# Reordering the opening of a fused attention and MLP kernel: x tiles first, warm-up at once, q two units ahead

## The chip, the cores and the metric

The kernel runs on one core of a Trainium2 chip. The metric is the device time of one execution in microseconds (us). A profile's span is some 1.8 us shorter than the time of the same execution (573.3 against 575.08 us before the change). Names: PE is TensorE (PEld its weight loads), DVE is VectorE, ACT is ScalarE, POOL is GpSimd, SP is SyncE, which here issues nearly all DMAs.

Each run reports its mean granted clock: 0.997 on a 573 us span means about 3.4 us at half rate, and the profile of the kernel before, with 0.997, has one such stretch of 3.41 us in its middle. The mean takes what comes before the first recorded change of the clock in a run as 1.00, even where the durations of the matmuls show half rate: in the kernel before the first change is at 13.42 us, and the stretch from 10.75 to 13.33 us reads 1.00 with its matmuls at 107 ns, against 55 ns later.

## The reference, cut to what matters

```python
mod = (silu(c) @ w_mod)              # six rows of 512: sa, ca, ga, sb, cb, gb
h = layernorm(x) * (1 + ca) + sa     # x: 2048 x 512
q = h @ wq                           # 32 heads of 128, 8 kv heads
p = softmax(q @ k.T * 128**-0.5)     # over the last 512 keys of the cache
x = x + ga * ((p @ v) @ wo)
h = layernorm(x) * (1 + cb) + sb
x = x + gb * (relu(h @ w1) @ w2)     # hidden size 1792
```

Inputs and output are bfloat16. The work is cut into 128 units: 4 blocks of 512 rows times 32 heads.

## The kernel before

In the timelines each engine starts its instructions in the order of the program text (PE before the change: column matmuls at 9.76 us, warm block at 10.61, then transposes and groups of four warm matmuls in turn from 13.13). The parts that the change and the argument touch:

```python
def warm(n):                          # matmuls on an identity tile, result unused
    for i in range(n):
        mm(bank[WBK][:, :P], ident[:, :], ident[:, :], True, True, [R_ident], [WBK], i == n - 1)

# --- opening ---
dma(c_col[:, :], c[0].rearrange("(c p) -> p c", p=P), "c", writes=[R_c], eng=ACT)
load_wm(1, ACT)                       # w_mod, two slices of 512 KB, on ACT's queue
load_wm(0, ACT)
for t in range(TPB):                  # four x tiles of 128 KB, on SP's queue
    dma(x_sb[:, t, :], xv[:, t, :], f"xa{t}", writes=[R_x[t]])
load_wq(0, 2)
load_k(0)
# ... POOL: ones, ident, constants; load_v(0); load_wq(2, 2)
silu()                                # DVE works on c first
for t in range(TPB):
    ln_stat(t)
ln_rstd(0)                            # one power on POOL for four tiles
for f in mod_cols_mm(0, QBK):         # 32 matmuls with one column each: silu(c) @ w_mod
    f()
mod_cols_evac(0, QBK)
warm(24)
for tl in range(TPB):
    ln_norm(tl)
    ln_tposes(tl, [0, 2])             # PE transposes of the normalized tile
    if tl < TPB - 1:
        warm(4)
ln_mod_ps([0, 2], hT[0], R_hT[0], 1)  # hT = xn.T * (1 + ca) + sa, on DVE and ACT
# ... more loads
q_mms(0)

# --- background loads, by step ---
add(60, load_w1)
add(64, load_w2)                      # two DMAs of 896 KB

# --- steady state ---
for s in range(NU):
    run_tasks(s, 100)
    # ... 
    s_mms(s, 0)                       # scores of unit s, first half; exp on ACT
    if s + 1 < NU:
        q_mms(s + 1)                  # q of the next unit; copy to qT on ACT
    s_mms(s, 1)
    if s >= 1:
        pv_mms(s - 1)                 # p @ v; DVE normalizes to o; DMA transposes o to oT
    pop_bg(4)                         # four matmuls of the output projection oT @ wo
```

## Time and profile before

| | value |
|---|---|
| time before the change | 574.68 us (573.48 to 574.73, 3 runs) |
| span of the profiled run | 573.3 us |
| PE busy | 551.1 us, 96% |
| first matmul | 9.76 us |
| first score matmul | 17.71 us |

The page of the kernel before. The first line is busy time, share and instruction count by engine. The other two show 40 slices of the span, in tenths: PE's busy share and the clock granted to it.

```profile
PE 551.1 (96%) x4082; PEld 316.8 (55%) x4157; DVE 242.8 (42%) x531; ACT 347.7 (61%) x445; POOL 38.2 (7%) x40
...
PE   3899999999999999989999999999999999999997
...
PEclk9999999999999999989999999999999999999999
```

PE is the bound (96% busy), and it is idle mainly at the start, up to 9.76 us. The table of waits, for PE (engine, tile, line, released by what: us in total, times, longest):

```profile
PE psQ L1350 <- DMA wmw<-in_w_mod_dram: 9.8, 1, 9.8
PE psW L1350 <- DMA oT<-o: 2.5, 1, 2.5
PE psS L1350 <- ACT qT L1455: 1.1, 2, 0.8
PE psQ L1350 <- ACT hT L1400: 0.9, 1, 0.9
...
```

PE waits 9.8 us for w_mod. The chain of waits through the opening (start us, duration us, what):

```profile
1.84 7.79 DMA wmw<-in_w_mod_dram
...
9.76 0.99 PE psQ L1350 x32
10.75 2.58 PE psW L1350 x24
13.34 0.33 PE psS L1353 x4
13.66 0.22 PE psW L1350 x4
...
15.04 0.79 ACT hT L1400
...
15.95 1.00 PE psQ L1350 x3
...
16.97 0.61 ACT qT L1455
...
17.71 0.61 PE psS L1350 x2
```

`psQ x32` are the column matmuls, `psW` the warm-up, `psS L1353` the transposes. The 24 warm matmuls cost 2.58 us on the path, 107 ns each. From 13.66 us a group of four takes 0.22 us, or 55 ns each: the array has come to full rate (the recorded change of the clock is at 13.42 us), and q0 (`psQ x3` and one more) runs at it.

### The profile page before, as it was taken

What the parts mean: (1) busy time and instruction counts of PE and PEld (TensorE: products, weight loads), DVE (VectorE), ACT (ScalarE), POOL (GpSimd) and SP (SyncE); (2) the same over time, 40 slices, a digit from 0 to 9 for tenths busy, and PEclk for the clock granted to TensorE, in tenths of its full rate; (3) what the DMA queues carried; (4) which work ended last, traced back from release to release, by engine and by line L of the source; (5) the groups of instructions that cost most, each with busy time, mean ns of one, the idle gap of its engine ahead of it and who ended that gap; (6) DMA issues with size and microseconds to landing.
All of it is one profiled execution on the core that took longest, in us unless ns stands there. A gap on an engine that the chain in (4) does not pass through costs nothing.

```text
span 573.3 us, 9628 instructions
## 1 busy us (share of the span) xinstructions
PE 551.1 (96%) x4082; PEld 316.8 (55%) x4157; DVE 242.8 (42%) x531; ACT 347.7 (61%) x445; POOL 38.2 (7%) x40
## 2 busy tenths in 40 slices
PE   3899999999999999989999999999999999999997
PEld 3466555555665555545555666555555554444443
DVE  3354465533333655323336553333354438321133
ACT  1877666777777666656777777666677744432400
POOL 1000000002300000013100000330000000000000
PEclk9999999999999999989999999999999999999999
DMA  8695859333231245541312341221123210210001
GB/s 224 179 203 111 194 105 190 67 83 43 40 76 37 38 83 121 166 102 37 71 41 41 76 78 38 38 38 38 37 38 69 47 35 0 39 37 23 22 27 46
DMA packets 111620, 42.67 MB, mean 74 GB/s; under 512 B 94032, under 2 KB 111184, under 8 KB 111568
## 3 DMA queue, kind: packets, MB, share of 16 engines
q1 hardware_dynamic: 109984, 40.92, 34.8%
q10 hardware_dynamic: 1584, 1.05, 0.6%
q8 instruction: 34, 0.56, 0.4%
q14 instruction: 18, 0.15, 0.1%
HBM read 18.35 MB, written 2.10 MB: 36 GB/s over the span
## 4 chain that ended last, share of the span: by engine, by line
PE 94%; DMA 3%; issue 1%; ACT 1%; DVE 0%; SPq 0%; ACTq 0%
PE psS L1350 27%; PE psO L1350 25%; PE psQ L1350 22%; PE psW L1350 19%; DMA wmw<-in_w_mod_dram 1%; DMA wmw<-in_B_w_dram 1%; DMA oT<-o 1%; SPq L1295 0%; ACT qT L1455 0%; ACT PT L1463 0%; PE psS L1353 0%; ACTq L1296 0%; ACT hT L1400 0%; DVE PT L1626 0%; DVE o L1474 0%
## 5 line engine op out<-in xcount | busy, mean ns | idle before, releaser
L1463 ACT ACTIVATE PT<-psS 128x1024 bf16<-128x1024 f32 x256 | 262.8, 1028 | 134.3 <-PE psS L1350 134.2
L1350 PE MATMUL psS<-qT,kT 128*128 128x512 bf16 x509 | 152.3, 381 | 1.3 <-ACT qT L1455 1.1
L1350 PEld LDWEIGHTS psO<-v,PT 128*128 128x128 bf16 x2048 | 126.7, 98 | 30.5 <-issue 0.5
L1350 PE MATMUL psO<-v,PT 128*128 128x129 bf16 x2048 | 137.0, 220 | 0.0
L1350 PE MATMUL psQ<-hT,wq 128*128 128x512 bf16 x511 | 132.2, 381 | 0.9 <-ACT hT L1400 0.9
L1350 PE MATMUL psW<-wo,oT 128*128 128x512 bf16 x451 | 118.0, 379 | 5.7 <-DMA oT<-o 2.5
L1473 DVE RECIPROCAL rinv<-psO 128x4 f32<-128x4 f32 x128 | 23.3, 182 | 236.2 <-PE psO L1350 236.2
L1474 DVE TENSOR_TENSOR o<-psO,rinv 128x512 bf16<-128x512 f32 x128 | 88.5, 691 | 4.4
L1350 PEld LDWEIGHTS psQ<-hT,wq 128*128 128x128 bf16 x512 | 50.3, 98 | 62.0 <-issue 2.0
L1350 PEld LDWEIGHTS psS<-qT,kT 128*128 128x128 bf16 x512 | 49.8, 98 | 60.6 <-issue 1.3
L1455 ACT ACTIVATE qT<-psQ 128x512 bf16<-128x512 f32 x128 | 75.8, 592 | 1.2 <-PE psQ L1350 1.2
L1350 PEld LDWEIGHTS psW<-wo,oT 128*128 128x128 bf16 x512 | 45.0, 98 | 35.7 <-DMA oT<-o 3.0
L1615 ACT ACTIVATE wq<-psS 128x512 bf16<-128x512 f32 x56 | 33.4, 597 | 49.7 <-PE psS L1350 49.7
L1496 DVE TENSOR_TENSOR acc<-psW,acc 128x512 f32<-128x512 f32 x48 | 33.1, 690 | 9.4 <-PE psW L1350 9.4
L1350 PE MATMUL psO<-wmw,wq 128*128 128x512 bf16 x136 | 31.0, 379 | 0.3
L1499 POOL TENSOR_TENSOR acc<-acc,gaf 128x512 f32<-128x512 f32 x12 | 15.2, 1269 | 173.1 <-DVE acc L1496 173.1
L1366 POOL TENSOR_TENSOR rstd<-rstd,cst 128x4 f32<-128x4 f32 x8 | 8.1, 1012 | 276.7 <-DVE rstd L1365 276.7
L1350 PE MATMUL psS<-h2T,wmw 128*128 128x512 bf16 x110 | 25.2, 379 | 0.1
L1350 PE MATMUL psS<-hT,wmw 128*128 128x512 bf16 x110 | 24.4, 379 | 0.1
L1626 DVE TENSOR_TENSOR PT<-psO,gbf 128x512 f32<-128x512 f32 x10 | 6.9, 691 | 40.2 <-PE psO L1350 40.2
L1350 PEld LDWEIGHTS psO<-wmw,wq 128*128 128x128 bf16 x140 | 13.7, 98 | 16.5
L1360 DVE BATCH_NORM_STATS2 st<-x 128x6 f32<-128x512 bf16 x32 | 21.7, 678 | 1.2 <-DMA x<-in_A_x_dram 1.2
(57 smaller groups left out, 162.2 us busy)
## 6 DMA issues: line engine op xcount, KB each, us to landing
wo<-in_A_wo_dram SPq DMA_DIRECT2D x4, 1024.0 KB, 6.0
wq<-in_A_wq_dram SPq DMA_DIRECT2D x7, 512.0 KB, 5.8
wmw<-in_B_w_dram SPq DMA_DIRECT2D x4, 896.0 KB, 5.3
wmw<-in_w_mod_dram SPq DMA_DIRECT2D x4, 512.0 KB, 4.5
oT<-o SPq DMA_TRANSPOSE x128, 2.4
out_dram<-PT SPq DMA_DIRECT2D x16, 128.0 KB, 1.7
x<-in_A_x_dram SPq DMA_DIRECT2D x3, 512.0 KB, 4.1
wmw<-in_w_mod_dram ACTq DMA_DIRECT2D x2, 512.0 KB, 7.1
```

Source lines behind the costliest of these rows:

```text
L1350: kb.op(PE, lambda e: e.matmul(out_ap, lhsT, rhs, start=start, stop=stop), reads=reads, group_writes=[R_b[k] for k in bk], signal=signal)
L1360: kb.op(DVE, lambda e: e.bn_stats(st[:, t, :], x_sb[:, t, :]), reads=[R_x[t]], writes=[R_st[t]])
L1366: kb.op(POOL, lambda e: e.tensor_tensor(rstd[:, sl], rstd[:, sl], cst[:, 0:1].to_broadcast([P, TPB]), op=ALU.pow), reads=[R_rstd[b], R_cst ...
L1455: kb.op(ACT, lambda e: e.activation(qT[u % NQT][:, :], bank[QBK], ACTF.Copy), reads=[R_b[QBK]], writes=[R_qT[u % NQT]])
L1463: kb.op(ACT, lambda e: e.activation(PT[u % NPT][:, pr * 2:pr * 2 + 2, :], s_ps[pr][:, :, :], ACTF.Exp, scale=scale), reads=[R_b[pr * 2], R ...
L1473: kb.op(DVE, lambda e: e.reciprocal(rinv[:, u, :], o_ps[:, :, P]), reads=[R_b[5], R_b[6]], writes=[R_rinv])
L1474: kb.op(DVE, lambda e: e.tensor_tensor(o_sb[u % NOS][:, :, :], o_ps[:, :, 0:P], rinv[:, u, :].unsqueeze(2).to_broadcast([P, TPB, P]), op=A ...
L1496: kb.op(DVE, lambda e: e.tensor_tensor(acc[:, tl, :], bank[WBK], acc[:, tl, :], op=ALU.add), reads=[R_b[WBK], R_acc[tl]], writes=[R_acc[tl]])
L1499: kb.op(eng, lambda e: e.tensor_tensor(acc[:, tl, :], acc[:, tl, :], gaf[:, :], op=ALU.mult), reads=[R_acc[tl], R_ga], writes=[R_acc[tl]])
L1615: kb.op(ACT, lambda e: e.activation(h1T[b % 2][:, fc, :], bank[bk], ACTF.Relu), reads=[R_b[bk]], writes=[R_h1[b % 2][fc]], pre=all_events( ...
L1626: kb.op(DVE, lambda e: e.tensor_tensor(yt[i], bank[bk], gbf[:, :], op=ALU.mult), reads=[R_b[bk], R_gb], writes=[R_yt[i]], pre=pt_done if c ...
```

## The change

The intent: put x in front of w_mod so that DVE's statistics start early, run the warm-up while PE has nothing else to do, normalize three tiles before the fourth is in, and compute q two units ahead so that scores never wait for the copy of q. The core of the diff:

```diff
-    NQT = 2
+    NQT = 3
 ...
-    def ln_rstd(b):
+    def ln_rstd(b, lo=0, hi=TPB):       # rstd may now be made for part of the tiles
 ...
+    QA = 2
 ...
-    load_wm(1, ACT)
-    load_wm(0, ACT)
     for t in range(TPB):
-        dma(x_sb[:, t, :], xv[:, t, :], f"xa{t}", writes=[R_x[t]])
+        dma(x_sb[:, t, :], xv[:, t, :], f"xa{t}", writes=[R_x[t]], eng=ACT if t % 2 else SP)
+    load_wm(1)
+    load_wm(0)
 ...
-    silu()
-    for t in range(TPB):
-        ln_stat(t)
-    ln_rstd(0)
+    warm(48)
+    ln_stat(0)
+    ln_stat(1)
+    silu()
+    ln_stat(2)
+    ln_rstd(0, 0, 3)
+    ln_stat(3)
+    ln_rstd(0, 3, 4)
+    for tl in range(3):
+        ln_norm(tl)
+        ln_tposes(tl, [0, 2])
     for f in mod_cols_mm(0, QBK):
         f()
+    ln_norm(3)
+    ln_tposes(3, [0, 2])
     mod_cols_evac(0, QBK)
-    warm(24)
-    for tl in range(TPB):
-        ln_norm(tl)
-        ln_tposes(tl, [0, 2])
-        if tl < TPB - 1:
-            warm(4)
     ln_mod_ps([0, 2], hT[0], R_hT[0], 1)
 ...
+    q_mms(0)
+    q_mms(1, 5)                          # q1 goes to another PSUM bank
-    q_mms(0)
 ...
-        if s + 1 < NU:
-            q_mms(s + 1)
+        if s + QA < NU:
+            q_mms(s + QA)
```

## The prediction

The sum in it came to 3.3 + 0.7 = 4.0 us, less 0.6 for the risk: 3.4 us off the 574.68 measured is about 571.3, put as 571.2. From 6 to 8 us the DMA moved 374 GB/s in the kernel before; ACT's queue (c and w_mod) moved 0.56 MB of it and SP's queue, with x, 0.19 MB. Matmuls went from 107 to 55 ns with the recorded change of the clock at 13.42 us, 3.66 us after the first one.

> **What bounds the kernel now.** TensorE. On the profile page PE is busy 551.1 of 573.3 us (96%), and the chain of waits is 94% PE. PE idle time is almost all at the two ends: PE's first matmul starts at 9.76 us (the waits table: 9.8 us for the w_mod DMA), and the timeline has the first score matmul at 17.71 us; from about 20.5 us the chain is PE back to back. Only the opening can give time back.
>
> **The opening before (chain and timeline).** w_mod lands at 9.63; 32 column matmuls 0.99; 24 warm matmuls 2.58 (107 ns each, half rate); transposes and 12 more warm matmuls to 15.02; hT evictions, q0 start at 15.95, its qT copy at 16.97, first scores 17.71, first exp 18.34. Beside it, the fourth x tile lands only at about 9.3 us (DVE waited 1.16 us for it), because x (0.5 MB) shares the DMA engines with 1 MB of w_mod.
>
> **After, step by step (estimates from these durations).**
> - [...] In the DMA view the stream really starts at 4.0 us (c's tiny elements land at 4.8) and 0.4 MB has moved by 5.6-5.8: x is all in by about 6. x plus w_mod, 1.57 MB, is reached at about 8.5: w_mod lands there, 1.1 us earlier; wq now queues behind it.
> - DVE: four stats at 0.69+0.18, silu in between (0.55), rstd add at about 7.5, POOL pow 1.02, three norms at 0.41 from about 8.8 to 10.0.
> - The 2.6 us warm block leaves the path (48 warm matmuls run from about 1.4 to 6.5 us, in idle time). The column matmuls now stand behind the third tile's transposes: about 10.2 to 11.2; evacuation 0.35; hT evictions start at about 11.6 against 15.04; first scores about 14.4, first exp about 15.0 against 18.34. Saved: 3.3 us.
> - q1 is computed in the 0.75 us in which PE waited for the first qT copy. One more q (0.86) is out of the way before the steady state. The first four steps are balanced between ACT (two exps of 1.02 and a copy of 0.6, 2.65 us) and PE (2.63), so this is collected only later, where output projection makes PE the bound: about 0.5 to 0.9 us. Later, q two ahead gives nothing: PE waited for qT 1.1 us in all.
>
> Sum: 3.3 + 0.7 = 4.0 us if the array is at full rate at q0.
>
> **The risk.** [...] matmuls went from 107 to 55 ns about 3.6 us after the first. Now PE goes idle between the warm block (about 6.3) and the first transposes (about 9.2). If that re-throttles, 1 to 3 us come back. I take 0.6 off for it.
>
> **What the profile would show.** x waits gone from DVE; hT evictions at 11 to 12 us; first scores at 13.5 to 15; the trace from unit 2 on shifted by 3.3 to 4 us; PE total busy unchanged apart from warm matmuls. Wrong if: wq or k lands after 12 us and q or scores wait for DMA (they now queue behind w_mod); PE is cold at q0; pow or the column matmuls end later than said.
>
> **Time.** 571.2 us, 80% range 569.3 to 573.5. Faster by over 2% (below 563.2) 0.01, same 0.98, slower 0.01.

## The result, and the profile after

| | before | after |
|---|---|---|
| median time, same rounds | 574.70 us (573.48 to 574.91, 4 runs) | 570.56 us (569.93 to 572.15, 4 runs) |
| ratio | | 0.9936, 95% interval 0.9912 to 0.9961 |
| span of the profiled run | 573.3 us | 568.2 us |
| first transposes | 13.13 us | 9.41 us |
| hT starts | 15.04 us | 12.20 us |
| first score matmul | 17.71 us | 16.26 us |

A ratio is the mean time of one kernel's runs over that of the other's of the same rounds, so it is not quite the ratio of the medians. The profiled run before took 575.08 us, more than any of its rounds, and the profiled run after was the fastest of its four; so the spans differ by 5.1 us and the medians by 4.1. The forecast of 571.2 us and its range hold. The profile shows that the way there was not the one forecast. The page after, the same lines:

```profile
PE 553.0 (97%) x4094; PEld 318.7 (56%) x4169; DVE 242.9 (43%) x532; ACT 347.3 (61%) x445; POOL 38.7 (7%) x41
...
PE   6999999999999999989999999999999999999997
...
PEclk8999999999999999999999999999999999999999
```

The low clock has left the middle and now stands in the first slice. PE's waits after:

```profile
PE psS L1353 <- DVE xn L1371: 3.0, 1, 3.0
PE psW L1350 <- DMA oT<-o: 2.1, 1, 2.1
...
PE psQ L1350 <- DVE hT L1397: 1.1, 1, 1.1
```

The wait for w_mod is gone. The first one here is PE idle between the warm block, over at 6.43 us, and the first transposes. The chain through the opening after:

```profile
9.41 1.46 PE psS L1353 x12
10.87 0.83 PE psQ L1350 x32
11.71 0.46 PE psS L1353 x4
...
12.21 1.01 DVE hT L1397 x2
...
13.28 1.49 PE psQ L1350 x3
14.77 1.65 PE psO L1350 x4
16.42 0.43 PE psS L1350 x2
```

hT comes 2.84 us earlier than before, yet the first scores only 1.45 us earlier. q1 (`psO x4`) takes 1.65 us, 412 ns per matmul, where the same four take 0.86 us in the steady state. Windows of two microseconds of the kernel after say why (window, length, busy time and count by engine, then the granted clock, the DMA share, GB/s; the clock is the third number from the end):

```profile
8.00:10.00 2.00, 0.59 (x6) 0.59 (x7) 1.93 (x7) 0.00 (x0) 1.55 (x2) 0.85 1.32 238
10.00:12.00 2.00, 2.00 (x45) 1.89 (x42) 0.55 (x3) 0.00 (x0) 0.00 (x0) 0.50 1.23 272
...
14.00:16.00 2.00, 2.00 (x6) 0.73 (x5) 0.00 (x0) 0.60 (x1) 0.00 (x0) 0.50 1.10 336
16.00:18.00 2.00, 2.00 (x10) 0.69 (x7) 0.00 (x0) 1.54 (x3) 0.00 (x0) 0.94 1.19 312
```

Read at 0.2 us, the clock was at half rate from 9.41 to 16.24 us. To see where along the run the time came from, take the start of each unit's DVE reciprocal, which follows its p @ v:

| | before, us | after, us | earlier by |
|---|---|---|---|
| unit 0 | 22.75 | 20.98 | 1.77 |
| unit 64 | 242.16 | 240.39 | 1.77 |
| unit 66 | 253.50 | 249.69 | 3.81 |
| unit 124 | 456.31 | 452.50 | 3.81 |
| unit 125 | 459.80 | 455.13 | 4.67 |
| last DVE instruction | 570.45 | 565.30 | 5.15 |

Nothing drifts: there are four steps. The opening gave 1.77. The q lead gave 0.86 at unit 125, where the last units have no q to compute. A step of 0.48 comes in the MLP near the branch that both kernels take there. It does not follow the change: from unit 125 to the last DVE instruction the fourteen profiles take 110.15 to 110.65 us, with the kernel before and a_w2late (new opening, below) both at 110.65 and b_w2late (old opening) at 110.15. And 2.04 us came at unit 65, which the change did not touch. There, windows of the kernel before:

```profile
246.00:248.00 2.00, 0.26 (x2) 0.00 (x0) 0.56 (x1) 0.00 (x0) 0.00 (x0) 1.00 1.16 328
248.00:250.00 2.00, 1.25 (x4) 0.56 (x5) 0.69 (x1) 0.00 (x0) 0.00 (x0) 0.74 0.60 121
250.00:252.00 2.00, 2.00 (x7) 0.63 (x6) 0.00 (x0) 1.22 (x2) 1.91 (x2) 0.50 0.00 0
252.00:254.00 2.00, 1.95 (x21) 1.39 (x21) 0.47 (x2) 1.42 (x2) 0.51 (x1) 0.91 0.00 0
```

and of the kernel after:

```profile
244.00:246.00 2.00, 0.50 (x3) 0.00 (x1) 0.76 (x2) 0.11 (x1) 0.00 (x0) 1.00 1.16 328
246.00:248.00 2.00, 1.37 (x7) 0.66 (x8) 0.69 (x1) 0.51 (x1) 0.17 (x1) 1.00 0.53 101
```

Both kernels stop PE there (2.49 and 2.14 us for the oT DMA), but only before did a stretch at half rate, from 248.94 to 252.36 us, follow. What PE waited for is seen in the timeline of the kernel before (start, duration, engine; SPq is SP issuing DMAs):

```profile
237.33 5.87 SPq L1296 DMA_DIRECT2D wmw<-in_B_w_dram  x2
...
243.25 4.53 SPq L1295 DMA_TRANSPOSE oT<-o  x3
...
248.75 0.46 PE L1350 MATMUL psW<-wo,oT 128*128 128x512 bf16 x1 [2.49 <-DMA oT<-o]
```

The two halves of w2 go out in front of the oT transpose of unit 63. SP holds back the second half until the first has landed, since both are declared as writers of the same w_mod buffers (SP's table of waits has up to 4.9 us for it); the oT transpose is issued only at 243.25 us, lands 5.46 us later, and the output projection of units 56 to 63 needs it.

Why half rate follows the wait in some runs only the traces do not settle; they give a hint. Within each run the recorded changes of the clock lie whole multiples of 3.413 us apart (in the kernel before at 13.42, 248.94 and 252.36 us, which is 69 times and once; in the kernel after 9.41 and 16.24 us, which is twice). To take them as points of a grid that runs on between them is the author's estimate. Of the 3.413 us up to the fall of the clock, PE was idle for 2.49 us in the kernel before (and for 2.68 and 2.63 us in a_keepwarm and a_nowarm, below). In the kernel after, the gap of 2.14 us lies across a point of that grid, with 1.70 us of it in one stretch, and in a_again the gap of 2.30 us lies so with 1.44; there the clock stayed. That would fit a cost of the wait that depends on where it falls; no run moves the same wait along the grid, so it is not shown.

### The profile page after: what moved, and what is told of

It is laid out like the page before. It is cut to its first block, busy times and chain, and to the rows that moved or that the text cites. A ratio compares the mean times of both kernels' runs of the same rounds, so it can differ in the third digit from the quotient of the medians.

```text
span 568.2 us, 9662 instructions
## 1 busy us (share of the span) xinstructions
PE 553.0 (97%) x4094; PEld 318.7 (56%) x4169; DVE 242.9 (43%) x532; ACT 347.3 (61%) x445; POOL 38.7 (7%) x41
## 4 chain that ended last, share of the span: by engine, by line
PE 96%; DMA 2%; DVE 1%; issue 1%; ACTq 0%
PE psS L1350 28%; PE psO L1350 26%; PE psQ L1350 23%; PE psW L1350 19%; DMA oT<-o 1%; DMA x<-in_A_x_dram 1%; DVE st L1360 0%; PE psS L1353 0%; DVE hT L1397 0%; DVE PT L1631 0%; DVE PT L1632 0%; DVE mv L1361 0%; DVE o L1475 0%; ACTq L1296 0%; DVE xn L1371 0%
## 5 line engine op out<-in xcount | busy, mean ns | idle before, releaser
L1350 PE MATMUL psQ<-hT,wq 128*128 128x512 bf16 x507 | 130.8, 381 | 1.1 <-DVE hT L1397 1.1
L1366 POOL TENSOR_TENSOR rstd<-rstd,cst 128x4 f32<-128x4 f32 (+2 forms) x9 | 8.6, 961 | 273.5 <-DVE rstd L1365 273.4
```

Of the source, the lines that this page charges most:

```text
L1350: kb.op(PE, lambda e: e.matmul(out_ap, lhsT, rhs, start=start, stop=stop), reads=reads, group_writes=[R_b[k] for k in bk], signal=signal)
L1366: kb.op(POOL, lambda e: e.tensor_tensor(rstd[:, sl], rstd[:, sl], cst[:, 0:1].to_broadcast([P, hi - lo]), op=ALU.pow), reads=R_rstd[sl] + ...
```

## The experiments

Two families, because the lottery at unit 65 (does half rate follow the wait or not) has to be taken out before small effects in the opening can be read: kernels named `a_` keep w2 where it is, kernels named `aw_` and `bw_` (and the two named `w2late`) load it at step 67. All are timed in five rounds against the kernel before on the same chip. All results were correct. "Unit 0" is the start of its reciprocal in the run's own profile.

| run | median us (range) | before, same rounds | ratio | mean clocks of the runs | unit 0 |
|---|---|---|---|---|---|
| a_again | 570.48 (570.41 to 571.54) | 575.00 | 0.9923 | 0.994 x4, 0.990 | 21.16 |
| a_keepwarm | 572.97 (572.42 to 575.00) | 575.00 | 0.9963 | 0.991 to 0.994 | 21.59 |
| a_nowarm | 573.82 (572.29 to 575.75) | 575.00 | 0.9973 | 0.996 to 1.000 | 21.56 |
| a_w2late | 568.50 (568.38 to 568.77) | 575.00 | 0.9883 | 0.994 x3, 0.991 | 21.63 |
| b_w2late | 570.93 (570.24 to 571.86) | 574.84 | 0.9930 | 1.000 x4, 0.999 | 23.81 |
| bw_qahead | 570.40 (569.25 to 570.68) | 574.84 | 0.9915 | 1.000 x4, 0.999 | 23.84 |
| aw_q1 | 570.02 (569.51 to 570.17) | 574.84 | 0.9915 | 0.991 x4, 0.990 | 22.03 |
| aw_dense | 566.52 (566.41 to 566.66) | 574.84 | 0.9853 | 1.000 x3, 0.999 | 19.51 |
| bw_xfirst | 571.13 (570.04 to 571.66) | 574.01 | 0.9950 | 1.000 x3, 0.999 x2 | 22.48 |
| aw_dense_clast | 566.89 (565.69 to 567.19) | 574.01 | 0.9871 | 0.996 to 1.000 | 19.77 |
| aw_dense_again | 566.62 (566.55 to 566.80) | 574.88 | 0.9857 | 1.000 x4 | 19.42 |
| aw_best | 567.08 (566.49 to 567.30) | 574.88 | 0.9863 | 1.000 x4 | 18.65 |

### The kernel after again (a_again)

No edit.

> The kernel after, unchanged, as the baseline of this batch. Theory [...]: times spread over about 570 to 572 us, and the profile again shows q0 and q1 at half rate (3 matmuls of q0 in about 1.5 us, 4 of q1 in about 1.65). Rival (the half rate in the profiled opening was an accident): q0 and q1 at full rate here, first scores at about 14.3 us instead of 16.26.

Half rate again, from 10.60 to 17.43 us, q0 1.49 us for three matmuls, q1 at 427 ns each, first scores at 15.68 us. Every one of the five runs has a clock of 0.994 or less, which by the mean clock is at least some 6.8 us at half rate; the profile has 6.83. The half rate in the opening is the kernel's habit and no accident of one profile. (The time sits where expected.)

### A longer warm block (a_keepwarm), and none (a_nowarm)

```diff
-    warm(48)
+    warm(88)      # a_keepwarm
+                  # a_nowarm: line removed
```

> 88 warm matmuls instead of 48, to cover the 3.0 us in which PE idled between warm block and transposes. Theory (that gap re-throttles the array and half rate is what the opening lost): clock granted stays full, first scores at 14.0 to 14.6 us instead of 16.26, first exp at about 15.0, whole kernel 1.6 to 2.2 us faster than a_again. Rival (the opening is paced by DMA landings and the DVE chain, not by PE's clock): first scores within 0.4 us of 16.26 and no gain in time.

> No warm matmuls at all. Theory (the block of 48 bought nothing because the array is throttled again before q0): within 0.4 us of a_again, first scores at 16.0 to 16.6 us. Rival (warming at once shortened the opening): first scores 1 us or more later and the kernel 1 us or more slower.

Timeline of a_keepwarm on PE:

```profile
1.41 6.52 PE L1350 MATMUL psW<-ident 128*128 128x128 bf16 x88 [1.41 <-POOL cst L1542]
9.50 1.04 PE L1353 MATMUL psS<-ident,xn 128*128 128x128 bf16 x12 [1.57 <-DVE xn L1371]
...
12.90 1.49 PE L1350 MATMUL psQ<-hT,wq 128*128 128x512 bf16 x3 [1.18 <-DVE hT L1397]
```

As forecasts of the time both missed. In a_keepwarm the block did bring the array to full rate (88 matmuls in 6.52 us), the gap before the transposes shrank from 3.0 to 1.57 us, and still the clock fell to half, from 11.27 to 18.10 us, and q0 took 1.49 us. First scores came at 15.89 us, within the range that the rival gave. So the one gap was not the whole cause. Of the 3.413 us up to the fall of the clock (7.86 to 11.27 us) PE was idle for 1.57 us, less than the 1.70 us that did no harm at unit 65 of the kernel after; nearly all the rest went to transposes and one-column matmuls. In the kernel after, PE spent 2.75 us of the 3.413 us from 9.41 us on such matmuls, and the clock stayed at half. Whether such matmuls had a part in it is not shown; no run separates them. In a_nowarm the first scores came at 16.22 us and unit 0 at 21.56 us, within 0.6 us of the kernel after: at the head of the kernel the block of 48 bought next to nothing, as the theory had it.

But both kernels were 2 to 3 us slower than a_again as a whole, which neither theory foresaw. The traces put that at unit 65: PE waits there 4.1 us in a_keepwarm and 3.5 us in a_nowarm, against 2.3 us in a_again, and both profiles show half rate behind it (250.20 to 253.62, and 249.80 to 253.22 us). Two timed runs of a_nowarm had a clock of 1.000 and still took 572.3 and 572.5 us, so half rate alone is not the reason. Why the wait is longer there is open.

### w2 out of the way (a_w2late, b_w2late)

```diff
-    add(64, load_w2)
+    add(67, load_w2)
```

> The load of w2 (1.8 MB) is issued at step 67 instead of 64, so that the oT transpose that unit 63's output projection waits for is not queued behind it. Theory (in both kernels PE idles about 2.1 to 2.5 us at unit 65 for that DMA, and [...] the array runs at half rate for 3.4 us, which costs about 2 us more, in some runs): wait of PE for the oT transpose gone, 2 to 2.5 us faster than a_again in each run without the drop and 4 to 4.5 us in each run with it, spread of the times smaller. Rival (the 2.0 us that the profile before lost at unit 65 is an effect of q order, absent after): gain of only the 2.1 us idle, spread unchanged.

> The kernel before with only the load of w2 moved from step 64 to 67. Theory (all 11 timed runs of before have a mean clock of 0.997, which is one half-rate window of 3.4 us, and it is the one at unit 65): PE's 2.5 us wait and the half-rate window both go, clock 1.000 in every run, 4.0 to 4.6 us faster than before, near 570.5. Rival (the window falls elsewhere, or the idle alone counts): clock stays 0.997 and the gain is 2.5 us, near 572.4.

In a_w2late the DMA issues stand the other way round (oT of units 62 to 65 first):

```profile
234.98 11.68 SPq L1295 DMA_TRANSPOSE oT<-o  x4
246.71 6.73 SPq L1296 DMA_DIRECT2D wmw<-in_B_w_dram  x2
```

PE's wait for oT is gone from the table of waits in both. a_w2late is 1.98 us faster than a_again in the same rounds, just under the 2 to 2.5 expected, and its spread falls from 1.1 to 0.4 us. The gain alone does not decide, since a_again had the wait without half rate behind it, at least in its profile, and the rival forecast nearly the same 2.1 us; the smaller spread speaks against the rival. b_w2late is 3.91 us faster than before in the same rounds, a little under the 4.0 to 4.6 expected, with clocks of 0.999 to 1.000: the half-rate stretch of before was indeed this one (3.41 us, from 248.94). In both, the wait went when the load of w2 was out of the way of oT.

One thing in b_w2late is not seen in its mean clock. Its column matmuls started at 9.83 us, 0.07 later than in the kernel before, but its unit 0 came at 23.81 us, 1.06 later. Groups of four matmuls still took 0.63 us in the middle of its opening:

```profile
14.48 0.63 PE L1350 MATMUL psW<-ident 128*128 128x128 bf16 x4
...
15.68 0.39 PE L1353 MATMUL psS<-ident,xn 128*128 128x128 bf16 x4
```

The first recorded change to full rate is at 15.57 us here and at 13.42 us in the profile before; in the other two kernels with the old opening it is at 16.05 (bw_qahead) and 13.21 us (bw_xfirst). So the profiled old opening varies by about 1 us with the moment at which full rate comes, and a step of 1 us in unit 0 between two single profiles proves nothing.

So unit 65 cost the kernel before 3.9 us and the kernel after 2.0 us. The difference, 1.9 us (3.91 less 1.98), is part of what the change seemed to gain, and it has nothing to do with the opening. How it divides between wait and half rate varies: of 36 timed runs of the kernel before, 23 had a clock of 0.997 and took 575.07 us on average, 11 had 1.000 and took 574.22. A run without half rate is only 0.85 us faster, so in such runs the wait must be longer than the profiled 2.5 us, or the opening slower, as in b_w2late; none of them was profiled. With unit 65 out of the way the change is worth 570.93 less 568.50, 2.4 us (in different rounds; 2.7 by the ratios).

### q two units ahead alone (bw_qahead), and the new opening without it (aw_q1)

```diff
 # bw_qahead, on b_w2late
-    NQT = 2
+    NQT = 3
 ...
     q_mms(0)
+    q_mms(1, 5)
 ...
-            q_mms(s + 1)
+            q_mms(s + QA)       # QA = 2
```

aw_q1 is a_w2late with the reverse: QA = 1, NQT = 2, no `q_mms(1, 5)`.

> b_w2late plus q two units ahead, old opening. Theory (the fill is paced by ACT, so one q less only counts where PE is the bound, collected at the last units): 0.86 us faster than b_w2late (0.7 to 1.1), PV of unit 0 not earlier than in b_w2late by more than 0.2 us, the gain appears after unit 124. Rival (q1 in the gap also shortens the opening by its 0.75 us): 1.5 us or more faster than b_w2late, with PV of unit 0 0.6 us earlier.

> The kernel after with w2 late (a_w2late, 568.5) but q only one unit ahead. Theory (lead worth 0.86 at the end, but at half rate q1 delays the first scores by about 0.7 us): first scores 0.5 to 0.8 us earlier than in a_w2late (16.14), whole kernel 0.2 to 0.9 us slower than a_w2late. Rival (q1 costs nothing in front of the first scores): first scores unchanged within 0.2 us and 0.86 us slower.

bw_qahead: unit 0 at 23.84 against 23.81 us, as the theory had it, but by luck: w_mod came 0.35 us later in this profile (column matmuls at 10.18 us). From the last transposes to unit 0 the three profiles of the old opening with q one ahead (before, b_w2late, bw_xfirst) take 8.13 to 8.14 us and bw_qahead 7.75, so the lead saved 0.38 us there. Set against b_w2late, it stays 0.03 us behind up to unit 124 and is 0.83 us ahead from unit 125: 0.86 us at the end, where the theory put it. The medians differ by 0.53 with overlapping ranges, the ratios by 0.15%, which is 0.86 us.

aw_q1: first scores at 15.66 us against 16.14, 0.48 us earlier, a hair under the expected range. Then q1, still at half rate, took 1.71 us behind them, and unit 0 was 0.40 us later than in a_w2late (its q0 had started 0.25 us later). As a whole it was 1.5 us slower (570.02 against 568.50, in other rounds; 1.26 us from unit 125 on between the profiles), more than the 0.2 to 0.9 expected. Here all five runs have a mean clock of 0.990 or 0.991, by which some 10 us were at half rate, against 0.994 and some 6.8 us in three of the four runs of a_w2late. The lead is worth at least its 0.86 us in either opening; the expectation that it costs the new opening something was wrong.

### PE kept busy up to q0 (aw_dense, aw_dense_again)

```diff
 # on a_w2late
-    warm(48)
+    warm(100)
 ...
     for tl in range(3):
         ln_norm(tl)
         ln_tposes(tl, [0, 2])
+        if tl < 2:
+            warm(4)
     for f in mod_cols_mm(0, QBK):
         f()
+    warm(8)
     ln_norm(3)
     ln_tposes(3, [0, 2])
+    warm(16)
```

> a_w2late with PE kept busy up to q0: warm block of 100, warm matmuls between the transposes, after the column matmuls and before q0. Theory ([...] half rate is what the opening lost): q0 at full rate (3 matmuls in 1.0 us instead of 1.49), first scores at 13.9 to 14.7 us instead of 16.14, 1.4 to 2.0 us faster than a_w2late, clock 0.999 to 1.000. Rival (filler delays the real work as much as it saves, or clock has no part): no gain, within 0.4 us of a_w2late.

> aw_dense repeated as the baseline of this batch, on whatever chip: 566.2 to 566.9 us. It repeats the finding that with PE kept busy q0 runs at full rate: first scores at 14.6 to 15.1 us.

Timeline of aw_dense on PE:

```profile
13.09 0.98 PE L1350 MATMUL psQ<-hT,wq 128*128 128x512 bf16 x3
13.91 1.03 PE L1350 MATMUL psO<-hT,wq 128*128 128x512 bf16 x4
14.85 0.59 PE L1350 MATMUL psS<-qT,kT 128*128 128x512 bf16 x2
```

q0 takes 0.98 us for its three and scores start at 14.85 us, 1.29 us earlier than in a_w2late, just outside the range I gave. Unit 0 is 2.12 us earlier. The kernel is 2.0 us faster (566.52 against 568.50, in other rounds; 1.7 us by the ratios), with no half rate behind the warm block, and the repeat agrees (566.62). Useless matmuls, 84 more of them, made the kernel faster: this shows that half rate is what the new opening lost, and that closing one gap in part was not enough to keep the clock (1.57 us of it were left in a_keepwarm; the longest wait of PE behind aw_dense's warm block is 0.92). Which of the fillers are needed no run separates. hT starts at 12.07 us in a_w2late and 12.18 in aw_dense, so the gain is made after it, by PE's rate (q0's three matmuls in 0.98 us instead of 1.49).

Against b_w2late in the same rounds, aw_dense is 4.4 us faster (570.93 less 566.52): the worth of the change and the filler together, against an old opening that itself comes to full rate only at some 13 to 16 us.

### Only the order of the first loads (bw_xfirst)

```diff
 # on b_w2late
-    load_wm(1, ACT)
-    load_wm(0, ACT)
     for t in range(TPB):
-        dma(x_sb[:, t, :], xv[:, t, :], f"xa{t}", writes=[R_x[t]])
+        dma(x_sb[:, t, :], xv[:, t, :], f"xa{t}", writes=[R_x[t]], eng=ACT if t % 2 else SP)
+    load_wm(1)
+    load_wm(0)
```

> b_w2late with only the order of the first loads changed as the change has it: x on two queues first, then w_mod on one. All else old (warm block in the middle, one rstd, q one ahead). Theory (the old opening waits for w_mod, landing at 9.7 to 10.2 us, and the order brings that landing forward by about 1 us): w_mod in hand at 8.5 to 9.0, column matmuls start about 1.0 us earlier, 0.7 to 1.2 us faster than b_w2late (570.9). Rival (order only helps x, which was not what PE waited for): column matmuls at 9.7 or later, no gain.

The column matmuls started at 9.44 us, waiting for w_mod, against 9.76 in before and 9.83 in b_w2late. My 8.5 to 9.0 was wrong. 571.13 us is no gain over b_w2late's 570.93, and by the ratios it is slower (0.9950 against 0.9930, other rounds and another chip). Its unit 0 is 1.33 us earlier than in b_w2late, but its profile is the fastest of its five runs and had full rate 2.36 us sooner, at 13.21 us, so this is not the order's doing. The rival is nearer: the order of loads by itself is worth 0.3 to 0.4 us at the column matmuls and nothing that the times show. It serves DVE; that this pays together with the new order on PE is an inference, since no run has the new order on PE without it.

### c behind x (aw_dense_clast, aw_best)

```diff
 # aw_dense_clast, on aw_dense; warm(100) becomes warm(72), warm(8) goes
-    dma(c_col[:, :], ...)                       # first on ACT's queue
     for t in range(TPB):
         dma(x_sb[:, t, :], ..., eng=ACT if t % 2 else SP)
+    dma(c_col[:, :], ...)                       # behind x
 ...
-    silu()                                      # after the second stat
 ...
     ln_stat(3)
+    silu()
     ln_rstd(0, 3, 4)
```

aw_best is the same, but all four tiles are normalized and transposed first, and silu and the column matmuls come after them, with warm matmuls between.

> aw_dense with the 2-byte-element load of c issued behind the x tiles instead of in front, silu after the fourth stat, warm block 72, no filler before the last transposes. Theory (c's 512 tiny elements hold up the x tile behind them, which lands only at 5.5 us): second stat starts at 4.0 to 4.7 us instead of 5.5, hT at 10.8 to 11.4 instead of 12.18, 0.8 to 1.4 us faster than aw_dense (566.5). Rival (x lands at 5.5 us for start-up reasons of the queues, not for c): second stat still at 5.3 to 5.7, and no gain beyond the 0.3 us of the removed filler.

> c loaded behind the x tiles again, but silu no longer in front of the norms on DVE, and the column matmuls behind all transposes. Theory (aw_dense_clast moved the second stat from 5.5 to 4.4 us but gave it back because c then landed at 8.6 and silu held up rstd and the norms): transposes start at 7.5 to 8.2 us, column matmuls at 9.4 to 9.8 (now held by w_mod and c), hT at 10.7 to 11.3 instead of 12.2, 0.8 to 1.5 us faster than aw_dense. Rival (w_mod or c landing later than 9.5 sets the pace): hT at 11.5 or later and no more than 0.5 us.

The load of c moves 512 elements of two bytes, read from memory with a stride. The trace of the kernel after holds 512 packets of two bytes, all on ACT's queue: one for each element. And c is dear beyond its 1 KB. DMA issues of the kernel after (KB each, us to landing):

```profile
c_col<-in_c_dram ACTq DMA_DIRECT2D x1, 1.0 KB, 3.6
```

and of aw_dense_clast:

```profile
c_col<-in_c_dram ACTq DMA_DIRECT2D x1, 1.0 KB, 6.9
```

With c behind, the second x tile was there by 4.37 us instead of 5.51, as the theory said; the two x tiles on ACT's queue took 3.2 us from issue to landing (median) instead of 4.6 in aw_dense. But c itself, now beside w_mod, landed only at 8.6 us, as the timeline of aw_dense_clast shows:

```profile
4.37 0.66 DVE L1360 BATCH_NORM_STATS2 st<-x 128x6 f32<-128x512 bf16 x1
...
8.62 0.21 ACT L1407 ACTIVATE tmp<-c_col 128x4 f32<-128x4 bf16 x1 [4.92 <-DMA c_col<-in_c_dram]
```

silu then held up the norms behind it on DVE, hT started at 12.44 us instead of the expected 10.8 to 11.4, and nothing was gained (566.89 us; by the ratios 0.9871 against aw_dense's 0.9853).

aw_best cured that. hT started at 11.32 us, 0.02 outside the expected range, and unit 0 came 0.77 us earlier than in aw_dense_again in the same rounds. The kernel as a whole was 0.46 us slower (567.08 against 566.62, ranges overlapping). The gain was given back at units 55 to 57 and 87 to 89, 0.62 and 0.57 us, a step which the table of waits of aw_best names:

```profile
PE psO L1350 <- DVE o L1475: 0.7, 2, 0.4
```

At those units DVE stands in order behind a norm of the next LayerNorm, which waits for the DMA transpose of the previous normalized tile (3.90 us at unit 55, 3.29 in aw_dense_again). The eviction of p @ v stands behind it, and PE behind the eviction. So a faster start met another DMA wait further on. aw_dense remains the fastest kernel, 8.3 us under before and about 4 us under the kernel after.

## Why the prediction was right or wrong

The number was right, 571.2 against 570.56 us, and that was luck: two large errors cancelled.

- **"Saved: 3.3 us" in the opening, and "first scores about 14.4".** Right about the path at full rate: from b_w2late to aw_dense the gain is 4.4 us, of which 0.86 is the q lead at the end, so 3.5 us for the opening, against the forecast 3.3 (by unit 0 it is 3.24 us from the profile before, from which the forecast was worked). But aw_dense holds 84 warm matmuls that the forecast did not have. In the change as it was made, scores came at 16.26 us and the opening gave 1.77 us.
- **"If that re-throttles, 1 to 3 us come back. I take 0.6 off for it."** The loss was named and its cost was in the stated range (1.7 to 2.0 us by aw_dense against a_w2late), but this is the mis-sized term: it was treated as a one-in-a-few risk, and it happened in every run of the kernel after (a clock of 0.994 or less in all nine). The cause named, the idle gap after the warm block, was only part of it: a_keepwarm nearly halved the gap (1.57 us instead of 3.0) and the clock still fell to half, for 6.83 us.
- **"PE idle time is almost all at the two ends ... Only the opening can give time back."** This is the step that failed. The waits table read for the forecast listed a 2.5 us wait for the oT DMA, and the page had a low slice of clock in the middle. Taking w2 out of the way gained 3.9 us before and 2.0 us after; the 1.9 us between them came to the change as a gift and made up for what half rate took.
- **"About 0.5 to 0.9 us" for q two ahead, collected late.** Right: 0.86 us at unit 125, and 0.86 in bw_qahead. The 0.38 us that it saved in the opening of bw_qahead was not forecast apart.
- **"w_mod lands there [8.5 us], 1.1 us earlier."** Wrong: column matmuls waited for it until 9.44 us in bw_xfirst, and in the kernel after its second half took 7.1 us from an issue at about 2.2, so it landed at about 9.3. It did not matter, because PE reached the column matmuls at 10.67 us.
- **Statistics, pow and norms "from about 8.8 us".** Right: norms from 8.93 us. But "x waits gone from DVE" was not so: DVE waited 1.33 us for the second tile, and the chain of waits runs through that load.
- **"The trace from unit 2 on shifted by 3.3 to 4 us."** Wrong: 1.77 us at unit 2. This check alone would have exposed the cancellation.

The sum that would have been right: 1.8 (opening at half rate) plus 0.9 (q lead) plus 1.9 (unit 65) is 4.6 us by the profiles and experiments, against 4.1 and 4.5 us measured in two sets of rounds; the 1.8 rests on one pair of profiles. Why the wait at unit 65 differs between kernels that do not differ there stays open.

## What to carry to other kernels

The warm-up block was worth here what the array's clock was when the real matmuls came: next to nothing in the kernel after (q0's three matmuls in 1.49 us, unit 0 within 0.6 us of a_nowarm's), and with the fillers of aw_dense 2.12 us at unit 0 against a_w2late (q0 in 0.98 us). So check the duration of the first real matmul, and try filling PE up to it as aw_dense did, across transposes, one-column matmuls and short waits, not only the first gap. Align two traces unit by unit before crediting a change with its total: a step far from the edited code is another cause, and it can hide a loss as well as add a gain. The big background load in front of a small urgent one cost PE a wait of 2.49 us here, and in some runs a stretch of 3.41 us at half rate behind it; moving the load three steps gained 3.9 us in the kernel before, nearly as much as the whole change.

## What the traces showed of the clock and of the load of c

- Of the 3.413 us up to the fall of the clock, 2.49, 2.63 and 2.68 us of PE idleness at unit 65 were followed by half rate (the kernel before, a_nowarm, a_keepwarm), and so were 2.07 us in the opening of a_w2late (warm block over at 5.61 us, fall at 7.68) and 1.57 us in that of a_keepwarm; 1.44 and 1.70 us in one stretch at unit 65 (a_again, the kernel after) were not. So no single length of idleness divides these cases.
- Half-rate stretches lasted 3.41 us (the kernel before), 6.83 us (the kernel after) and 10.24 us (a_w2late), and in a_keepwarm their starts, 11.27 and 250.20 us, lie 70 times 3.413 us apart. One of 3.41 us cost about 1.9 us at unit 65 of the profiled run before (4.35 us lost there against a_w2late, 2.49 of it the wait).
- The granted clock of a profile reads 1.00 before its first recorded change, which is at 13.42 us in the kernel before. Its 24 warm matmuls ran at 107 ns each in windows that show a clock of 1.00. Durations had to be read for the start of the kernel.
- The x tiles on ACT's queue took 4.6 us to landing behind c in aw_dense and 3.2 in front of it in aw_dense_clast. c itself took 3.6 us to landing in the kernel after and 6.9 in aw_dense_clast, where it was issued behind x and beside w_mod.
